# Order of transfers and decoding steps before the first attention slot, and a finished row of w3 @ w_out in three slots instead of two

## The chip, the cores and the metric

The kernel runs on one core of a Trainium2 chip. The metric is the device time of one execution in microseconds (us). The core has a matrix engine (TensorE, PE in the profile, with its weight loads as PEld), a vector engine (VectorE, DVE), a scalar engine (ScalarE, ACT), a general engine (GpSimd, POOL) and a queue engine (SyncE, SP) that here issues all transfers. Each engine runs its own instructions strictly in order and waits for the others by semaphores. Matrix products are accumulated in PSUM banks; everything else lies in SBUF.

## The reference

Three stages follow each other: clustered attention over 2 x 8 heads of 768 x 64, a product MLP, and a second MLP with softplus.

```python
mask = q_assign[:, :, :, None] == k_assign[:, :, None, :]   # nearest of 16 centroids, by head
scores = np.where(mask, scale * np.matmul(q, k.transpose(0, 1, 3, 2)), -1000000000.0)
attn = np.exp(scores - np.max(scores, axis=-1, keepdims=True))
attn = attn / (np.sum(attn, axis=-1, keepdims=True) + 1e-09)
x = np.matmul(attn, v)               # (1536, 512) after the heads are put side by side
h = (x @ w1) * (x @ w2) @ w3         # w1, w2: 512 x 1024; w3: 1024 x 1024
y = h @ w_out                        # w_out: 1024 x 512
g = softplus(y @ w_in)               # w_in: 512 x 2048
out = g @ w_o2                       # 2048 x 512
```

The MLP weights come as float64. The kernel reads them as pairs of 32-bit words and builds float32 from them.

## The kernel before

**Attention in slots.** Heads are taken in eight pairs. The loop `for s in range(NSLOT + ML + AL)` has 106 slots, six for each of the 16 heads and ten more for the lag. Slot s computes the scores of 128 queries against all keys on PE (`mx_pe`, line 592), takes their extremum on DVE (`mx_red`, line 601), and, nine slots behind, computes the scores transposed (`st_pe`, line 622), their exponential on ACT (`st_exp`, line 629) and, one slot further behind, the product with v (`av_pe`, line 637). The score buffers `mbank` and `sbank` are single: `mx_pe` of a slot waits for the reduction of the slot before, `st_pe` for the exponential of the slot before.

**Preparation of the next pair.** The tables `PE` and `EV` lay the work for pair pi over the slots of the pairs before it, by slot minus 12 pi. This text calls s modulo 12 the position. Position 0 loads q and k (`load_qk`); 4 to 7 square and sum them on POOL and DVE; 8 to 11 turn q and k on PE and copy them on ACT into the tiles H and L (`t1_pe`, `t1_ev`, lines 299 and 310), half j = 0 in 8 and 9, half j = 1 in 10 and 11. Position 9 also has `norm_root` (lines 274 and 275) on ACT. Positions 1 to 5 of the next twelve compare with the centroids, and 7 ends with `back_pe` and `back_ev` (tile sg). The copies from H, L and sg into the operands of the score products are transfers on SP: `t_dma(pi, j)` has seven, `m_dma(pi, j)` two. They stand at position 4 (`t_dma` for j = 0) and 8 (`m_dma` 0, `t_dma` 1, `m_dma` 1: eleven transfers in a row). H and L have one buffer for each j, so `t1_ev` of a pair for j = 1, at position 10, waits until `t_dma` for j = 1 of the pair before has been read out.

**The product w3 @ w_out.** Beside the attention the kernel computes w3 @ w_out once, in 24 jobs n (`wseq`): four halves-of-w_out rows ("o"), eight w3 rows ("3"), and the same again for the second half g = 1. Job n begins at step k = 3n, and one step runs in each slot. The table `WT` says which letter runs at which step after 3n: A, b, c, d decode a weight (A on ACT, b, c, d on DVE; d also issues the next load, since three raw buffers are there); s splits w_out on ACT and POOL; T turns w3 on PE (line 488); h and l split it on ACT and DVE; m is the accumulation on PE (`w3_acc`, line 507, 12 products); p adds the first half's row on DVE for g = 1 (`w3_add`, line 515); q copies the leading part on ACT (`w3_out`, tiles w3oh and w3p); e takes the remainder on DVE and gives the PSUM bank back (`w3_end`). Within a slot the letters h, l, p, q, e come after `mx_red` and before `st_exp`; A, b, c, d, s after `st_exp`; T and m at the end of the slot. The bank for T, m and the turns of the preparation is one of three (`rbank`), taken first in, first out.

**Before the first slot.** A hand-written list prepares pair 0 and loads weights; then eight rounds `r` from -20 to -13 prepare pair 1, with one decoding step each (`w_next`), and further steps follow until `wk[0]` is 14. So slot 0 starts at step 14 and slot s runs step s + 14. When `wk[0]` reaches `NWSTEP` = 82 (slot 67) the first three weights of the first MLP are loaded (`feed.load(3)`, 1.5 MB, tile w12r); they are decoded later by `feed.take`.

Of the kernel before, what the change touches and what calls it, by code (L numbers as in the profile page):

```python
# [22 lines left out]
def f32(ap):  # L23
    return ap.bitcast(F32)
# [3 lines left out]
def fused_kernel(ctx: ExitStack, tc, q, k, v, centroids, w1, w2, w3, wo, w_in, w_o2, out):  # L28
# [11 lines left out]
    QC = S // P  # L40
# [33 lines left out]
    def load_w(pl, src, cols, name):  # L74

        wide = src.dtype != F32
        t = pl.tile([P, 1024], I32, tag="raw", name=name)
        if not wide:
            t = t.bitcast(F32)[:, :512]
        tv = t if cols is None else t.rearrange("p (c f) -> p c f", c=cols)  # L80
        dma_in(tv, src.bitcast(I32) if wide else src)
        return t
# [103 lines left out]
    def load_qk(pi):  # L186
        if pi >= NPAIR:
            return
        b, h0 = divmod(2 * pi, H)
        r = ap1.tile([P, 2, QC, 2, D], F32, tag="rawqk", name=f"rawqk{pi}")  # L190
        for ni, src in enumerate((q, k)):
            for j in range(2):
                dma_in(r[:, j, :, ni, :], src[b, h0 + j].rearrange("(p c) d -> p c d", p=P))
        QK[pi] = r

    def centroid_load():
        PR["cw"] = ap1.tile([P, D], F32, name="cw")
        dma_in(PR["cw"], centroids.rearrange("h c d -> (h c) d"))

    def centroid_prep():  # L200
        cw = PR["cw"]
        sq = ap1.tile([P, D], F32, name="csq")
        s = ap1.tile([P, 8], F32, name="cs")
        nc.scalar.activation(sq, cw, AF.Square, accum_out=s[:, 0:1])
        nc.gpsimd.tensor_tensor(
            out=s[:, 1:2], in0=s[:, 0:1], in1=half_c, op=ALU.pow
        )

        nc.vector.tensor_scalar_max(s[:, 2:3], s[:, 1:2], 1e-30)
        nc.vector.reciprocal(s[:, 3:4], s[:, 2:3])  # L210
        nc.vector.scalar_tensor_tensor(
            out=s[:, 4:5], in0=s[:, 3:4], scalar=s[:, 0:1], in1=s[:, 2:3],
            op0=ALU.mult, op1=ALU.add,
        )
        nc.vector.tensor_scalar(
            out=s[:, 5:6], in0=s[:, 4:5], scalar1=0.5, scalar2=1e-6,
            op0=ALU.mult, op1=ALU.add,
        )
        nc.vector.reciprocal(s[:, 6:7], s[:, 5:6])
        cn = PR["cn"] = ap1.tile([P, 2, D], F32, name="cn")  # L220
        for i in range(2):
            nc.vector.tensor_scalar(
                out=cn[:, i, :], in0=cw, scalar1=s[:, 6:7], scalar2=None, op0=ALU.mult
            )
# [22 lines left out]
    def norm_sq(pi, j):  # L247
        sq = ring.tile([P, QC, 2, D], F32, tag="w3k", name=f"sq{pi}_{j}")
        if pi >= 2:
            nc.gpsimd.tensor_tensor(out=sq, in0=QK[pi][:, j], in1=QK[pi][:, j], op=ALU.mult)  # L250
        else:
            nc.scalar.activation(sq, QK[pi][:, j], AF.Square)
        PR["sq", j] = sq
# [63 lines left out]
    def t_dma(pi, j):  # L317

        hd = 2 * pi + j
        a, l = f32(PR["H", j]), f32(PR["L", j])
        qt = QT[hd] = apT.tile([P, 2, S], F32R, tag="q", name=f"q{hd}")
        kt = KT[hd] = apT.tile([P, 2, S], F32R, tag="k", name=f"k{hd}")
        nc.gpsimd.memset(f32(kt[96:97, 1, :]), 1.0)
        dma = nc.sync.dma_start
        dma(f32(qt[:D]), a[:D].unsqueeze(1).to_broadcast([D, 2, S]))
        dma(f32(kt[:D, 0, :]), a[D:])
        dma(f32(kt[:D, 1, :]), l[D:])
        for n in range(2):  # L330
            dma(f32(qt[D : D + 32, n, :]), l[32 * n : 32 * n + 32])
            dma(f32(kt[D : D + 32, n, :]), a[D + 32 * n : D + 32 * n + 32])
# [78 lines left out]
    def m_dma(pi, j):  # L411
        for ni, d in enumerate((QT, KT)):
            o = 64 * ni + 32 * j
            nc.sync.dma_start(f32(d[2 * pi + j][96:, 0, :]), f32(PR["sg"][o : o + 32, :]))
# [9 lines left out]
    NW = len(wseq)  # L424
    wnext = [0]

    def w_load():
        n = wnext[0]
        if n < NW:
            k, i, g = wseq[n]  # L430
            if k == "o":
                r = g * NK + i
                src = wo[r * P : (r + 1) * P, :]
            else:
                src = w3[i * P : (i + 1) * P, g * 512 : (g + 1) * 512]
            W3["r", n] = load_w(raws, src, None, f"w3r{n}")
            wnext[0] += 1
# [90 lines left out]
    def w3_end(n):  # L528
# [7 lines left out]

    WT = {
        "o": {0: "Ab", 1: "c", 2: "d", 5: "s"},
        "3": {0: "Ab", 1: "c", 2: "d", 3: "T", 4: "hl", 7: "m", 8: "pq", 9: "e"},
    }  # L540
    WF = {
        "A": w_scale, "b": lambda n: w_bits(n, 0), "c": lambda n: w_bits(n, 1),
# [4 lines left out]
    def w_step(k, kinds):  # L547
        for n in range(max(0, k // 3 - 3), min(NW, k // 3 + 1)):
            for x in WT[wseq[n][0]].get(k - 3 * n, ""):
                if x in kinds:  # L550
                    WF[x](n)
# [3 lines left out]
    def load_v(pi):  # L555

        if pi < NPAIR:
            b, h0 = divmod(2 * pi, H)
            for j in range(2):
                t = xp.tile([P, QC, 2 * D], F32, tag="x", name=f"v{pi}_{j}")  # L560
                nc.gpsimd.memset(t[:, :, D * (1 - j) : D * (2 - j)], 1.0)
                dma_in(
                    t[:, :, D * j : D * j + D], v[b, h0 + j].rearrange("(p c) d -> p c d", p=P)
                )
                V[2 * pi + j] = t
# [16 lines left out]
    NH = B * H  # L582
    NSLOT = NH * QC
    ML = 9
    AL = 1
# [90 lines left out]
    def x_norm(u):  # L676
        g, hf = divmod(u, 2)
        b, h = divmod(g, H)
        if b not in XT:
            XT[b] = xp_.tile([P, CC, S], F32, tag="x1", name="xT1")  # L680
        rs = slice(D * (h % 2), D * (h % 2) + D)
        cs = slice(hf * HALF, (hf + 1) * HALF)
        nc.gpsimd.tensor_tensor(  # L683
            out=XT[b][rs, h // 2, cs],
            in0=TT.pop(u)[rs], in1=R[g // 2][rs, cs], op=ALU.mult,
        )
# [137 lines left out]


    WALL = "AbcdsThlmpqe"
    W0 = 14
    wk = [0]

    def w_next(kinds=WALL):  # L830
        w_step(wk[0], kinds)
        wk[0] += 1

    with tc.manual_schedule():
        centroid_load()
        load_qk(0)
        for _ in range(3):
            w_load()
        load_v(0)
        centroid_prep()  # L840
        t1_pe(0, 0)
        t1_pe(0, 1)
        t1_ev(0, 0)
        norm_sq(0, 0)
        t1_ev(0, 1)
        centroid_turn()
        t1_pe(0, 2)
        t1_pe(0, 3)
        t1_ev(0, 2)
        norm_sq(0, 1)  # L850
        t1_ev(0, 3)
        t_dma(0, 0)
        t_dma(0, 1)
        load_qk(1)
        load_v(1)
        norm_sum(0, 0)
        sims_pe(0, 0)
        sims_ev(0, 0)
        norm_sum(0, 1)
        norm_root(0)  # L860
        sims_pe(0, 1)
        sims_ev(0, 1)
        w_next()
        norm_rec(0, 0)
        norm_rec(0, 1)
        simsT_pe(0)
        w_next()
        norm_rec(0, 2)
        w_next()
        assign(0, 0)  # L870
        assign(0, 1)
        w_next()
        back_pe(0)
        back_ev(0)
        m_dma(0, 0)
        m_dma(0, 1)
        for r in range(-20, -2 * QC):
            steps(PE, r + 2 * QC)
            steps(EV, r + 2 * QC)
            if wk[0] < W0:  # L880
                w_next()
        while wk[0] < W0:
            w_next()
        for s in range(NSLOT + ML + AL):
            j = s - ML
            a = j - AL
            if s < NSLOT:
                mx_pe(s)
                mx_red(s)
            if s and s % QC == 0 and s <= NSLOT:  # L890
                m_row(s // QC - 1)
            w_step(wk[0], "hlpqe")
            if a > 0 and a % 3 == 0:
                av_ev(a // 3 - 1)
            steps(PE, s)
            steps(EV, s)
            if 0 <= j < NSLOT:
                st_pe(j)
                st_exp(j)
            w_step(wk[0], "Abcds")  # L900
            if 0 <= a:
                av_pe(a)
            w_step(wk[0], "Tm")
            wk[0] += 1

            for g in range(NH):
                r = s - (ML + AL + QC * g + QC - 1)
                if r in (2, 4, 6):
                    r_ev(g, r // 2 - 1)
                if r == 8:  # L910
                    x_norm(2 * g)
                    x_norm(2 * g + 1)
            if wk[0] == NWSTEP:
                feed.load(3)
                assert s < ML + AL + QC * NH // 2 + QC + 6
            if s == NSLOT + 1:
                feed.take(2)
                taken += 2
# [179 lines left out]
```

## Time and profile before

| | us |
|---|---|
| median of 3 runs | 882.47 (881.14 to 884.43) |
| profiled execution | 882.9 |
| its span | 881.1 |
| PE busy | 813.7 (92%) |
| DVE busy | 498.7 (57%) |
| ACT busy | 413.2 (47%) |
| POOL busy | 242.8 (28%) |
| first reduction of slot 0 begins | 42.70 |
| last reduction of slot 95 begins | 367.3 |

The busy share of PE says little by itself, since a product on half the clock is busy twice as long. The page's line PEclk gives the granted clock in tenths of full speed in 40 slices of 22 us; its two levels are 1.2 and 2.4 GHz (0.50 and 1.00). Views used below: the waits (who waited for whom), the timeline (instructions in order of time with the idle time before them and what ended it), the windows (busy time and granted clock of a stretch), and the chain (the work that ended last, followed back).

### The profile page before, as it was taken

What the parts mean: (1) busy time and instruction counts of PE and PEld (TensorE: products, weight loads), DVE (VectorE), ACT (ScalarE), POOL (GpSimd) and SP (SyncE); (2) the same over time, 40 slices, a digit from 0 to 9 for tenths busy, and PEclk for the clock granted to TensorE, in tenths of its full rate; (3) what the DMA queues carried; (4) which work ended last, traced back from release to release, by engine and by line L of the source; (5) the groups of instructions that cost most, each with busy time, mean ns of one, the idle gap of its engine ahead of it and who ended that gap; (6) DMA issues with size and microseconds to landing.
All of it is one profiled execution on the core that took longest, in us unless ns stands there. A gap on an engine that the chain in (4) does not pass through costs nothing.

```text
span 881.1 us, 11317 instructions
## 1 busy us (share of the span) xinstructions
PE 813.7 (92%) x4033; PEld 704.9 (80%) x4033; DVE 498.7 (57%) x903; ACT 413.2 (47%) x763; POOL 242.8 (28%) x249
## 2 busy tenths in 40 slices
PE   4289999899999699989999999999979999999998
PEld 3167777677777577759999999998878999899886
DVE  6585657585755455439642324775996445445442
ACT  3325454444444444455542423665556545545543
POOL 2431215241414111145410011342443222222221
PEclk9579999899999899999999999999999999999999
DMA  9774455654535634036410111450200000000001
GB/s 225 171 191 133 116 145 140 159 147 105 126 82 114 156 82 109 11 101 202 155 48 10 41 48 48 147 189 1 96 24 1 37 1 1 37 1 0 36 1 37
DMA packets 77832, 76.47 MB, mean 87 GB/s; under 512 B 46416, under 2 KB 62928, under 8 KB 77776
## 3 DMA queue, kind: packets, MB, share of 16 engines
q1 hardware_dynamic: 77776, 75.75, 31.8%
q8 instruction: 32, 0.52, 0.2%
q14 instruction: 24, 0.20, 0.1%
HBM read 50.41 MB, written 3.24 MB: 61 GB/s over the span
## 4 chain that ended last, share of the span: by engine, by line
PE 72%; DVE 11%; DMA 6%; issue 4%; ACT 3%; SPq 2%; POOL 2%; DVEq 0%; ACTq 0%; POOLq 0%
PE avb L637 11%; PE sb L622 6%; PE mb L1027 6%; PE sb L784 6%; PE rb L784 6%; PE sb L983 6%; PE rb L983 6%; PE rb L507 4%; PE mb L592 3%; PE mb L806 3%; PE rb L1027 3%; PE avb L1027 3%; DMA q<-H 2%; PE rb L806 2%; PE avb L806 2%
## 5 line engine op out<-in xcount | busy, mean ns | idle before, releaser
L601 DVE TENSOR_REDUCE mn<-mb 128x1 f32<-128x768 f32 x96 | 91.6, 954 | 110.4 <-PE mb L592 110.0
L637 PE MATMUL avb<-E,v 128*128 128x384 f32 x384 | 144.7, 500 | 0.0
L66 POOL TENSOR_TENSOR ln<-ln,u 128x384 f32<-128x384 f32 x64 | 67.1, 1050 | 179.3 <-DVE ln L1007 173.8
L622 PE MATMUL sb<-q,k 128*128 128x384 f32 (+1 forms) x384 | 92.0, 362 | 19.2 <-ACT E L629 19.2
L629 ACT ACTIVATE E<-sb 128x768 f32<-128x768 f32 x96 | 77.6, 808 | 50.0 <-PE sb L622 49.0
L637 PEld LDWEIGHTS avb<-E,v 128*128 128x128 f32 x384 | 73.1, 195 | 28.1 <-issue 2.4
L622 PEld LDWEIGHTS sb<-q,k 128*128 128x128 f32 (+1 forms) x384 | 67.5, 195 | 26.6 <-ACT E L629 23.7
L592 PE MATMUL mb<-k,q 128*128 128x384 f32 x192 | 70.4, 449 | 12.2 <-DVE mn L601 11.4
L983 PE MATMUL sb<-ys,wh_i 128*128 128x384 f32 x256 | 72.5, 344 | 7.5 <-ACT t L994 6.9
L983 PE MATMUL rb<-ys,wh_i 128*128 128x384 f32 x256 | 70.6, 337 | 0.0
L784 PE MATMUL sb<-xs,wh 128*128 128x384 f32 x256 | 68.6, 339 | 1.7 <-DVE ab L793 1.7
L784 PE MATMUL rb<-xs,wh 128*128 128x384 f32 x256 | 68.0, 336 | 0.0
L996 DVE TENSOR_SCALAR u<-t 128x384 f32<-128x384 f32 x64 | 24.3, 379 | 73.1 <-ACT t L995 72.7
L592 PEld LDWEIGHTS mb<-k,q 128*128 128x128 f32 x192 | 36.0, 200 | 33.1 <-DVE mn L601 15.8
L983 PEld LDWEIGHTS sb<-ys,wh_i 128*128 128x128 f32 x256 | 47.7, 191 | 11.6 <-ACT t L994 8.9
L66 POOL TENSOR_TENSOR wl_o<-d_o,wh_o 128x512 fp32r<-128x512 f32 x16 | 20.8, 1301 | 127.8 <-ACT wh_o L61 124.2
L1004 DVE SCALAR_TENSOR_TENSOR u<-u,t 128x384 f32<-128x384 f32 x64 | 37.6, 588 | 23.7 <-ACT ln L1002 23.5
L784 PEld LDWEIGHTS sb<-xs,wh 128*128 128x128 f32 x256 | 46.3, 188 | 3.5 <-DVE ab L793 2.3
L683 POOL TENSOR_TENSOR xT<-t,R 64x384 f32<-64x384 f32 x32 | 34.3, 1090 | 49.9 <-DMA R<-rd 43.7
L983 PEld LDWEIGHTS rb<-ys,wh_i 128*128 128x128 f32 x256 | 46.9, 188 | 1.3
L784 PEld LDWEIGHTS rb<-xs,wh 128*128 128x128 f32 x256 | 46.5, 188 | 0.1
L1002 ACT ACTIVATE ln<-u 128x384 f32<-128x384 f32 x64 | 33.3, 520 | 24.7 <-DVE u L996 24.4
(178 smaller groups left out, 1884.4 us busy)
## 6 DMA issues: line engine op xcount, KB each, us to landing
w3r<-in_moe_w_dram SPq DMA_DIRECT2D x16, 512.0 KB
w12r<-in_moe_w_dram SPq DMA_DIRECT2D x16, 512.0 KB
wir<-in_moe_w_in_dram SPq DMA_DIRECT2D x16, 512.0 KB
wor<-in_moe_w_out_dram SPq DMA_DIRECT2D x16, 512.0 KB
q<-H SPq DMA_DIRECT2D x16, 384.0 KB
w3r<-in_moe_w_out_dram SPq DMA_DIRECT2D x8, 512.0 KB
rawqk<-in_q_dram SPq DMA_DIRECT2D x16, 192.0 KB
rawqk<-in_k_dram SPq DMA_DIRECT2D x16, 192.0 KB
```

Source lines behind the costliest of these rows:

```text
L66: nc.gpsimd.tensor_tensor(out=o, in0=i, in1=hi, op=ALU.subtract)
L507: nc.tensor.matmul(m, a[:, ks], bb, start=(mc == 0 and x == 0), stop=(mc == NK - 1 and x == 2))
L592: nc.tensor.matmul(mbank[:, hf, :HALF], QT[g][:, 0, c * P : (c + 1) * P], KT[g][:, 0, hf * HALF : (hf + 1) * HALF], start=True, stop=True,)
L601: nc.vector.tensor_reduce(out=MN[g][:, c : c + 1], in_=mbank[:, :, :HALF], op=ALU.min, axis=AX.XY)
L622: nc.tensor.matmul(sbank[:, i, :HALF], KT[g][: P - 31 * n, n, ks], QT[g][: P - 31 * n, n, qs], start=(n == 0), stop=(n == 1),)
L629: nc.scalar.activation(E[j], sbank[:, :, :HALF], AF.Exp, scale=-1.0)
L637: nc.tensor.matmul(avbank[:, :HALF], V[g][:, 2 * kp + i, :], e[:, i, :], start=(kp == 0 and i == 0), stop=(kp == 2 and i == 1),)
L784: nc.tensor.matmul(bk[:, :BLK], a[:, sl], bb, start=(n == 0), stop=(n == 3 * CC - 1))
L806: nc.tensor.matmul(ybank[e][:, :BLK], a[:, es], bb, start=(fc == 0 and n == 0), stop=(fc == NFC - 1 and n == 2),)
L983: nc.tensor.matmul(hbank[(bl * NF2 + fc) % 4][:, :BLK], a[:, sl], bb, start=(n == 0), stop=(n == 3 * CC - 1))
L1004: nc.vector.scalar_tensor_tensor(out=u, in0=u, scalar=-1.0, in1=t, op0=ALU.add, op1=ALU.subtract)
L1027: nc.tensor.matmul(ob, a[:, sl], bb, start=(fc == 0 and n == 0), stop=(fc == NF2 - 1 and n == 2),)
```

## The change

- Before the first slot: two weights are loaded at first instead of three, and v of pair 0 not there. `load_qk(1)` moves ahead of `t_dma(0, 1)`, which itself moves behind `m_dma(0, 0)`. The third weight and `load_v(0)` come after `m_dma(0, 1)`, and `load_v(1)` after the rounds.
- Only A and b of job 0 stay ahead of the rounds. `W0` becomes 9: slot s runs step s + 9, five steps less than before, and every letter of the stream moves by five slots.
- The letters p, q and e of a finished row stand at steps 8, 9 and 10 instead of 8, 8 and 9.
- One assertion goes and one is added; they issue nothing.

```diff
-        "3": {0: "Ab", 1: "c", 2: "d", 3: "T", 4: "hl", 7: "m", 8: "pq", 9: "e"},
+        "3": {0: "Ab", 1: "c", 2: "d", 3: "T", 4: "hl", 7: "m", 8: "p", 9: "q", 10: "e"},
...
-    W0 = 14
+    W0 = 9
...
         centroid_load()
         load_qk(0)
-        for _ in range(3):
-            w_load()
-        load_v(0)
+        w_load()
+        w_load()
         centroid_prep()
...
         t_dma(0, 0)
-        t_dma(0, 1)
         load_qk(1)
-        load_v(1)
...
         sims_ev(0, 1)
-        w_next()
         norm_rec(0, 0)
         norm_rec(0, 1)
         simsT_pe(0)
-        w_next()
         norm_rec(0, 2)
-        w_next()
+        w_step(0, "A")
+        w_step(0, "b")
         assign(0, 0)
         assign(0, 1)
-        w_next()
         back_pe(0)
         back_ev(0)
         m_dma(0, 0)
+        t_dma(0, 1)
         m_dma(0, 1)
+        w_load()
+        load_v(0)
+        wk[0] = 1
         for r in range(-20, -2 * QC):
             steps(PE, r + 2 * QC)
             steps(EV, r + 2 * QC)
             if wk[0] < W0:
                 w_next()
-        while wk[0] < W0:
-            w_next()
+        load_v(1)
```

## Rows read from the trace of the kernel before

**Rows 1.** The page, granted clock in 40 slices of the span.

```profile
PEclk9579999899999899999999999999999999999999
```

**Rows 2.** Waits of PE from 64 to 400: us in total, times, longest us.

```profile
PE sb L622 <- ACT E L629: 19.2, 12, 6.7
PE mb L592 <- DVE mn L601: 0.8, 2, 0.5
```

**Rows 3.** Timeline of PE, three stretches: start us, us, what, in brackets idle before.

```profile
163.09 1.65 PE L622 MATMUL sb<-q,k 128*128 128x384 f32 x4 [2.73 <-ACT E L629]
...
205.82 0.97 PE L622 MATMUL sb<-q,k 128*128 128x384 f32 x4 [2.07 <-ACT E L629]
...
305.28 1.65 PE L622 MATMUL sb<-q,k 128*128 128x384 f32 x4 [6.73 <-ACT E L629]
```

**Rows 4.** Windows: stretch and length in us, busy by engine, PEclk, DMA share, GB/s.

```profile
19.20:49.90 30.70, 10.86 (x40) 8.57 (x40) 19.34 (x32) 11.37 (x21) 11.86 (x13) 0.50 0.83 187
...
162.50:169.40 6.90, 6.32 (x16) 4.91 (x17) 4.39 (x8) 2.65 (x5) 2.47 (x4) 0.51 0.26 90
206.90:210.40 3.50, 3.50 (x11) 2.33 (x10) 0.86 (x3) 1.72 (x3) 1.11 (x3) 0.51 0.40 151
302.50:309.40 6.90, 4.12 (x9) 2.91 (x10) 2.16 (x4) 2.56 (x4) 3.11 (x6) 0.51 0.21 45
```

**Rows 5.** Timeline of ACT in the same stretches.

```profile
161.75 0.58 ACT L310 ACTIVATE H<-rb,qkcol 128x384 fp32r<-128x384 f32 x1 [3.69 <-DMA k<-H]
...
202.36 0.60 ACT L61 ACTIVATE w3oh<-rb 128x512 fp32r<-128x512 f32 x1 [5.15 <-DVE rb L515]
...
297.65 0.70 ACT L63 ACTIVATE w12r<-w12r 128x512 f32<-128x512 f32 x1 [1.72 <-DMA w12r<-in_moe_w_dram]
303.95 0.58 ACT L310 ACTIVATE H<-rb,qkcol 128x384 fp32r<-128x384 f32 x1 [5.59 <-DMA k<-sg]
```

**Rows 6.** Timeline of SP in the first and the last of these stretches.

```profile
152.58 0.56 SPq L414 DMA_DIRECT2D q<-sg  x1
...
158.92 0.59 SPq L332 DMA_DIRECT2D k<-H  x1
...
288.72 1.74 SPq L81 DMA_DIRECT2D w12r<-in_moe_w_dram  x3
```

**Rows 7.** Chain of work in order of time, from 64 on: start us, us, what.

```profile
72.10 0.44 PE rb L488 x4
...
73.22 0.72 PE sb L622 x4
73.93 1.29 PE avb L637 x4
75.23 2.78 PE rb L507 x12
...
158.92 2.72 DMA k<-H
...
392.38 4.63 DMA w12r<-in_moe_w_dram
```

**Rows 8.** Timeline of all engines from 14 to 67, the start.

```profile
14.28 0.60 SPq L332 DMA_DIRECT2D k<-H  x1
...
22.02 0.90 ACT L408 ACTIVATE sg<-rb,bigcol 128x768 fp32r<-128x768 bf16 x1 [5.59 <-PE rb L402]
...
27.76 0.57 SPq L414 DMA_DIRECT2D q<-sg  x1
27.83 0.84 ACT L252 ACTIVATE sq<-rawqk 128x768 f32<-128x768 f32 x1 [4.91 <-DMA rawqk<-in_k_dram]
...
36.47 0.42 DVE L457 TENSOR_SCALAR w3r<-w3r 128x512 int32<-128x512 int32 x1
...
42.70 0.95 DVE L601 TENSOR_REDUCE mn<-mb 128x1 f32<-128x768 f32 x1
...
66.58 0.94 PE L622 MATMUL sb<-q,k 128*128 128x384 f32 x4
```

More of the change, by code (lines that the diff above doesn't have):

```diff
@@ L679, in x_norm @@
         if b not in XT:
+            assert wk[0] > 3 * NW + 4
             XT[b] = xp_.tile([P, CC, S], F32, tag="x1", name="xT1")
@@ L914, in fused_kernel @@
                 feed.load(3)
-                assert s < ML + AL + QC * NH // 2 + QC + 6
             if s == NSLOT + 1:
```

## The prediction

> **What bounds the kernel now.** I read the page first. PE is busy 92% of the span (the table above), and in most of the 40 slices its clock is at or near full [rows 1]; from the first slots on the kernel is bound by PE, and a gain can come only from PE's idle time, from its time at half clock, or from what lies ahead of the stretch that PE fills. So the next view is PE's waits from 64 us on: 19.2 us in 12 waits of the transposed scores for the exponential before, 0.8 us for the reduction, and nothing else [rows 2]. The timeline shows that four of the 12 hold most of it: 2.73, 2.07 and 6.73 us [rows 3], and at 255.94 one that repeats the second to the digit; counted along the 96 reductions of line 601 these are slots 35, 46, 58 and 71. Three of the four are followed by a stretch at 0.51 of the clock, in which PE was busy 6.32, 3.50 and 4.12 us [rows 4]; at full clock the same work takes half, so they cost 3.16, 1.75 and 2.06 us more. The four, with their clock, are the prize: A = 2.73 + 3.16 = 5.9, B = 2.07 + 1.75 = 3.8, B' = 2.07, C = 6.73 + 2.06 = 8.8, in all 20.6 us.
>
> Then ACT in these stretches, because each wait is for an exponential. ACT runs in order, so what it waited for just before is the cause. In A it waited 3.69 us to write H, for `t_dma` to have read the old one; in C 5.59 us for the same kind of thing; in B it waited 5.15 us for the sum p of line 515 before the copy q, and the exponential stood behind q [rows 5]; B' has the same row 50 us later. SP shows why the transfers were late: in A the eleven transfers of position 8 start at 152.58, and the last of `t_dma` is issued at 158.92 [rows 6] and lands 2.72 us later [rows 7]. In C the three weights of `feed.load(3)`, 1.5 MB, are issued at 288.72, right ahead of the eleven [rows 6].
>
> **The change part by part.**
>
> *p, q, e in three slots (B, B').* Before, the accumulation m ends a slot; in the next, p waits for DVE's reduction, which waits for PE's scores behind m; q waits for p on ACT; the exponential waits behind q. That is the 5.15 us. With q one slot later its operand is long there, and p comes behind a reduction that waits for the same PE work, so DVE waits no longer than it did. Cost of the move: none of instructions; e gives the bank back one slot later, which is weighed below. B and B' go: -5.9 us. Next late there is the exponential's own scores, which PE itself sets.
>
> *Five steps later (C).* `feed.load(3)` moves from slot 67 to 72, position 0, behind `m_row`'s transfer of that slot. Until position 4 of the next pair only small transfers and v follow on SP, so the eleven of slot 68 have a free queue. C goes: -8.8. What is left there: ACT still meets one early decode of w12r, for which it waited 1.72 us [rows 5]. It should move along with the load and wait again, now with nothing else late: +1.7 (from 0 to the 5.6 of the row below it).
>
> *Five steps later (A).* The accumulations, 2.78 us each [rows 7], stood in slots 2 modulo 3, thus at positions 2, 5, 8, 11; now in 1 modulo 3, at 1, 4, 7, 10. One at 7 lets SP begin the eleven while PE is still in 7; one at the end of 10 fills PE while the exponential is late. Jobs 12 to 15 have none, so slots without accumulation were 27 to 40 and will be 32 to 45. Slot 34 (now with one in 31) and slot 46 (now with one of its own) each get 2.78 us of cover against a wait of 2.73. I take A as gone, -5.9, and leave 1.6 us for remnants in slots 34, 46 and 70 (none, to the whole 5.9 if the lag moves with the slots).
>
> *The start.* Before, pair 1's q and k are there at 27.83 and the copies of sg are issued at 27.76, though sg is ready at 22.92 [rows 8]: both stand in SP behind `t_dma(0, 1)`, weights and v. Now load_qk(1) follows `t_dma(0, 0)`, issued by 14.88 [rows 8], and needs about 5 us (4.63 for the slowest of the nearest kind [rows 7]): some 7 us earlier. On the other side `t_dma(0, 1)` waits in SP behind sg, and the third weight behind it. sg, with about 0.5 us of decoding less ahead of it, at 22.4; then eleven issues (nine took 6.9 from 152.58 to 159.51 [rows 6], so 8.5), load issued at 30.9, landed 2.7 to 4.6 later (the two transfers of [rows 7]): 33.6 to 35.5. ACT and DVE need it for job 2 and stand in line behind it with the last two turns. From the like point, 36.47, to slot 0 at 42.70 [rows 8] DVE needed 6.2 us, of which two steps (1.1) now come later: slot 0 at 38.7 to 40.6, say 39.2, 3.5 us earlier. (Not earlier at all if the squares of pair 1 have to wait for the buffer of sg, which SP now empties last: 42.7.) Slots 0 to 8 took 23.9 us, 42.70 to 66.58 [rows 8], with two accumulations among them, of which the later stood on the path: 23.9 - 2.8 = 21.1. PE's full stretch then begins at 60.3, 6.3 earlier. But two accumulations and two turns (0.44 each [rows 7]) that lay in the thin start now lie in the full stretch: 2 x (2.78 + 0.44) = 6.4. Net 0, from -4 to +5.
>
> Its clock is part of that span: between 19.2 and 49.9 it stood at 0.50, with PE busy 10.86 of 30.70 us [rows 4], and rose only after some dense us in slots 1 to 3. With two accumulations less the slots up to 8 are thinner. The Trainium skill ("TensorE: Matmul & The Clock Gate", "What's actually happening") says the gate follows how busy PE has lately been, and only knows half and full. The trace agrees in these stretches. By that rule the full stretch could begin at half clock, which this change makes likelier; a stretch like the one in A would then cost 3.2 us, an estimate from that row.
>
> *Rest.* The bank: in the second half the accumulation of job n takes the bank that e of job n-1 gives back early in the same slot. PE has 0.72 + 1.29 us [rows 7] of other products between the scores and it, DVE a reduction of 0.95 [rows 8] and e (0.6, as q [rows 5]), so e is done in time unless DVE is late; remnants +0.5. Each of the moved decoding letters keeps its neighbours; nothing is added. The MLP stages keep their order: 0, within 2 us either way.
>
> **Sum.** -20.6 + 1.7 + 1.6 + 0.5 + 0 = -16.8. The profiled span of 881.1 becomes 864.3; the execution took 882.9, 1.8 more, so 866.1; the median was 0.4 below that execution: 865.7. I say 865.5.
>
> **The rivals.**
>
> 1. *SP's lag moves with the slots.* The transfers at position 8 are still eleven, and ACT still waits for them at 10. If the cover by accumulations does not reach, A stays (5.9) and the decode of w12r costs up to 5.6 instead of 1.7: 865.5 + 5.9 - 1.6 + 3.9 = 874. For it: eleven issues of 0.6 to 0.7 us each are longer than two slots. Against: of the slots at position 10 with an accumulation beside the eleven, none is among the four waits except through q. Chance 0.13.
>
> 2. *The start gives nothing and costs.* Slot 0 not earlier (buffer of sg), and the full stretch begins at half clock: 865.5 + 3.5 + 3.2, about 872. Chance 0.10.
>
> 3. *Slower: e becomes the wait.* With one slot more, the bank is free only after DVE's reduction and e in the slot of the next accumulation. By the terms above PE reaches that accumulation 2.0 us after the scores and DVE ends e 1.6 us after them; it decides once DVE starts a slot more than 0.4 us late. If DVE were 2 us late in the seven slots of jobs 17 to 23, PE would stand 7 x 2 us, each followed by 1.75 of clock as in B: +26, thus 892. Against: PE waited for the reduction only twice, 0.8 us in all [rows 2]. Chance 0.05.
>
> 4. *It does not do what it says:* the waits only change place, each as large as before, with 6.4 us of PE work moved against an earlier start of the same size. 880 to 884. Chance 0.06.
>
> **How the numbers follow.** My forecast, 857 to 872, has 0.66. The 8 in 10: from 856 (remnants zero, start -4, and some of the small waits gone too) to 879, which takes in rivals 1 and 2. Faster by over 0.5% (about what a measurement of this kernel tells from no change) means below 878.1: forecast, rivals 1 and 2, less a little for costs that add up, 0.86. Within: 0.08. Slower, above 886.9: 0.06.
>
> **What would show it.** Right: in PE's waits from 64 to 400 the 19.2 us fall to about 5; ACT has no copy w3oh waiting 5 us for line 515; no stretch of half clock inside the attention slots after the start; `feed.load(3)` in slot 72 with PE going on; the first reduction near 39 and the first transposed scores near 60. Wrong in A: H waits over 3 us at slot 46 or 34 with PE idle behind it. Wrong in the start: first reduction at 42 or later. Wrong in the bank: line 507 waits for DVE. What I least trust is the landing of the third weight and where the early decode of w12r stands.

## The result and the profile after

The changed kernel takes 867.38 us in the median (867.09 to 868.11, 4 runs) against 883.3 (881.14 to 884.43, 4 runs) for the kernel before, measured beside it; the ratio is 0.9824, interval 0.9802 to 0.9846. The prediction was 865.5, with 856 to 879 as its range.

The waits of PE from 64 to 400 (us in total, times, longest), which answer to [rows 2]:

```profile
PE sb L622 <- ACT E L629: 8.7, 8, 2.3
PE avb L637 <- issue: 1.0, 2, 0.5
PE avb L637 <- ACT t L61: 0.4, 1, 0.4
```

The 19.2 us for the exponential are 8.7, and half of these lie behind the last slot. Two lines are new: the product with v of line 637 waits, which it did not before.

The timeline of PE at slots 35, 46, 71 and behind the last slot (start, us, what, idle before):

```profile
160.99 0.97 PE L622 MATMUL sb<-q,k 128*128 128x384 f32 x4 [1.10 <-ACT E L629]
...
194.12 1.53 PE L637 MATMUL avb<-E,v 128*128 128x384 f32 x4 [0.48 <-issue]
...
291.22 0.98 PE L622 MATMUL sb<-q,k 128*128 128x384 f32 x4 [1.28 <-ACT E L629]
...
361.63 0.97 PE L622 MATMUL sb<-q,k 128*128 128x384 f32 x4 [1.97 <-ACT E L629]
...
370.36 0.98 PE L622 MATMUL sb<-q,k 128*128 128x384 f32 x4 [2.28 <-ACT E L629]
```

Of [rows 3], the 2.73 of slot 35 is 1.10 and the 6.73 of slot 71 is 1.28; of the two waits of 2.07 at slots 46 and 58 nothing is left at the exponential. At slot 46, and likewise at 58, the product with v waits 0.48 instead.

The windows (busy time by engine, then the granted clock, DMA share, GB/s), which answer to [rows 4]:

```profile
50.70:60.90 10.20, 6.96 (x26) 5.04 (x27) 9.48 (x17) 2.91 (x5) 7.22 (x7) 0.50 0.80 181
60.90:371.50 310.60, 300.24 (x1407) 230.90 (x1407) 189.05 (x317) 150.92 (x255) 86.41 (x100) 1.00 0.49 123
371.50:375.00 3.50, 3.50 (x9) 2.58 (x8) 2.16 (x4) 1.29 (x3) 0.74 (x1) 0.51 0.00 0
```

From 60.9 to 371.5 the clock never falls. The three stretches of half clock inside the slots are gone; one ends the thin start, one lies behind the last slot. The kernel before had such stretches there too: 60.2 to 63.6, and 377.6 to 381.0, both at 0.50.

Where the time went, stretch by stretch: the beginnings of the scores of line 592, counted slot by slot in the two traces, and of the last product with v.

| from, to | before, us | after, us | difference | prediction |
|---|---|---|---|---|
| start to slot 32 | 150.50 | 150.19 | -0.3 | 0 |
| slot 32 to 38 (A) | 23.74 | 18.32 | -5.4 | -5.4 |
| slot 38 to 68 (B, B') | 114.53 | 111.94 | -2.6 | -4.9 |
| slot 68 to 72 (C) | 19.95 | 12.57 | -7.4 | -8.3 |
| slot 72 to 95 | 57.76 | 57.43 | -0.3 | +1.7 |
| slot 95 to the last product with v | 26.43 | 27.80 | +1.4 | 0 |
| rest | 488.20 | 487.43 | -0.8 | 0 |
| span | 881.1 | 865.7 | -15.4 | -16.8 |

(The 1.6 of remnants is shared here among slots 34, 46 and 70, and the 0.5 for the bank stands with B, B'.) The sum was missed by 1.4 us, but the terms less evenly: two were too good by 2.3 and 0.9, one cost did not come (1.7), and the stretch behind slot 95 is 1.4 longer. That the total came so close is in part luck, since these errors have both signs.

Each figure of the table is from one execution, and the runs below have further profiles of the same stretches. Slots 32 to 38 took 22.4 in three runs that keep the accumulations where they were (e1, e2, e3): half clock lasted 3.4 us there instead of 6.8. So A is worth 4.0 to 5.4. Slots 38 to 68 took 113.2 and 112.9 in two runs with the old letters at the old place (e2, e3), with both waits of 2.07 and no half clock behind them. So B and B' are worth 0.9 to 2.6. C is firm: it took 20.4 in e1 and e3, which leave the loads in slot 67, so the gain is 7.4 to 7.9. The 1.4 behind slot 95 is not the change's: a second profile of the changed kernel (e11) has 26.45 there, before 26.43.

### The profile page after: what moved, and what is told of

It is laid out like the page before. It is cut to its first block, busy times and chain, and to the rows that moved or that the text cites. A ratio compares the mean times of both kernels' runs of the same rounds, so it can differ in the third digit from the quotient of the medians.

```text
span 865.7 us, 11313 instructions
## 1 busy us (share of the span) xinstructions
PE 809.1 (93%) x4033; PEld 701.2 (81%) x4033; DVE 499.8 (58%) x903; ACT 411.4 (48%) x763; POOL 244.7 (28%) x249
## 4 chain that ended last, share of the span: by engine, by line
PE 78%; DVE 9%; issue 5%; ACT 3%; SPq 2%; DMA 1%; POOL 1%; ACTq 0%; DVEq 0%; POOLq 0%
PE avb L637 12%; PE sb L981 7%; PE mb L1025 7%; PE sb L622 7%; PE rb L981 6%; PE sb L785 6%; PE rb L785 6%; PE rb L507 5%; PE mb L592 4%; PE mb L807 3%; PE avb L1025 3%; PE rb L1025 3%; PE rb L807 2%; PE avb L807 2%; PE rb L345 1%
## 5 line engine op out<-in xcount | busy, mean ns | idle before, releaser
L637 PE MATMUL avb<-E,v 128*128 128x384 f32 x384 | 141.6, 490 | 1.6 <-issue 1.0
L637 PEld LDWEIGHTS avb<-E,v 128*128 128x128 f32 x384 | 71.0, 190 | 30.6 <-ACT t L61 2.3
L592 PE MATMUL mb<-k,q 128*128 128x384 f32 x192 | 69.4, 444 | 15.4 <-DVE mn L601 15.4
```

Source lines behind the costliest of these rows:

```text
L592: nc.tensor.matmul(mbank[:, hf, :HALF], QT[g][:, 0, c * P : (c + 1) * P], KT[g][:, 0, hf * HALF : (hf + 1) * HALF], start=True, stop=True,)
L637: nc.tensor.matmul(avbank[:, :HALF], V[g][:, 2 * kp + i, :], e[:, i, :], start=(kp == 0 and i == 0), stop=(kp == 2 and i == 1),)
```

## The experiments

My theory was the sum's own: four waits with their clock, each gone for its own reason, and a start that balances. The rivals were that one common cause (five slots later) does it all, or that the new order of transfers at the start does. Times are medians, and ratios are to the kernel before, measured beside each group. The runs are numbered e1 to e11.

**The parts of the change alone (the kernel before: 881.66).**

The letters only (e1):

```diff
-... 8: "pq", 9: "e"},
+... 8: "p", 9: "q", 10: "e"},
```

> The kernel before with p, q, e at steps 8, 9, 10 and nothing else. My theory (the copy q waited for the sum p on ACT, and two exponentials stood behind it): the two PE waits at slots 46 and 58 go, 2 x 2.07, and the 1.75 of half clock behind the first, 5.9 in all, less about 1 for what stands next: 877 to 879 against 883. Rival (the split does nothing alone, the waits went because the letters moved to other slots): 882 to 884.

Measured: 878.76, ratio 0.9962 (0.9935 to 0.9988). The timeline of PE at slots 46, 53 and 58:

```profile
203.44 0.80 PE L622 MATMUL sb<-q,k 128*128 128x384 f32 x3 [0.86 <-ACT E L629]
...
233.32 0.50 PE L507 MATMUL rb<-woh,w3th 128*128 128x512 f32 x1 [0.96 <-DVE w3ol L69]
...
251.70 0.62 PE L622 MATMUL sb<-q,k 128*128 128x384 f32 x2 [0.86 <-ACT E L629]
```

The theory had the right kind and the wrong size. Each 2.07 falls to 0.86, no stretch of half clock follows, and slots 38 to 68 are 3.3 us shorter (111.24 against 114.53); against e2 and e3, which have the two waits without half clock, 1.6 to 2.0. The median moved by 2.9 instead of 4 to 6. The row between shows rival 3 of the prediction in small: one accumulation waits 0.96 us for e. It stays at one.

The three loads only, in slot 72 (e2):

```diff
-            if wk[0] == NWSTEP:
+            if s == 72:
                 feed.load(3)
```

> The kernel before with the three loads of the first MLP's weights in slot 72 instead of 67, nothing else. Theory (the loads stood ahead of the eleven transfers of position 8): the wait of 6.73 at slot 71 falls to what is left in the kernel after there (1.3) up to a wait as in slot 35 (2.7), with less or no half clock: 5 to 7.5 faster, 876 to 878. Rival (the eleven transfers themselves are the wait, as in slot 35): 4.5 to 6 remain of 8.8, so 879 to 881.

Measured: 875.25, ratio 0.9916 (0.9888 to 0.9943), thus 6.4 faster. PE's wait at slot 71:

```profile
299.24 0.97 PE L622 MATMUL sb<-q,k 128*128 128x384 f32 x4 [1.32 <-ACT E L629]
```

The 1.5 MB ahead of the eleven transfers were the cause of C, and the rival falls: without them 1.32 us is left, not a wait as in slot 35.

The order of transfers only (e3: the new list before the rounds, but fourteen steps before slot 0 and the old letters; the edit is shown against the changed kernel):

```diff
-... 8: "p", 9: "q", 10: "e"},
+... 8: "pq", 9: "e"},
...
-    W0 = 9
+    W0 = 14
...
+        while wk[0] < W0:
+            w_next()
         load_v(1)
```

> The new order of transfers before the first slot, with fourteen steps before slot 0 and the letters as before. Theory: slot 0 as late as before, near 43, because five more decoding steps stand on DVE behind the third weight; the four waits stay in slots 35, 46, 58, 71: 881 to 885. Rival (the order itself brings a gain at the start of 3 us or more): first reduction at 40 or earlier, 879 or less.

Measured: 882.87, ratio 1.0012 (0.9987 to 1.0037): no difference. DVE's timeline at the first reduction:

```profile
42.61 0.52 DVE L457 TENSOR_SCALAR w3r<-w3r 128x512 int32<-128x512 int32 x1
43.23 0.69 DVE L461 SCALAR_TENSOR_TENSOR w3r<-w3r 128x512 int32<-128x512 int32 x1
43.84 0.95 DVE L601 TENSOR_REDUCE mn<-mb 128x1 f32<-128x768 f32 x1
```

Slot 0 begins at 43.84, 1.1 later than before [rows 8], with decoding right up to it. It is no later than in e2 (43.77), whose start is that of the kernel before: two profiles of one start differ by as much. So the new order brings slot 0 no nearer by itself.

The steps and letters only, in the old order of transfers (e4):

```diff
-... 8: "pq", 9: "e"},
+... 8: "p", 9: "q", 10: "e"},
...
-    W0 = 14
+    W0 = 9
```

> The old order of transfers, with nine steps before slot 0 and the new letters. Theory: the five steps fewer bring the earlier start and move the accumulations and the loads, so this has nearly all of the gain: first reduction near 39, waits at 35, 46, 58, 71 gone, 866 to 869. Rival (the new order of transfers is needed for the gain at the start): first reduction at 42 or later and 870 or more.

Measured: 869.0, ratio 0.9851 (0.9807 to 0.9894), which overlaps the interval of the whole change. Its first reduction stands earlier than in the changed kernel (38.01 against 39.76), and slot 35 looks the same:

```profile
38.01 0.94 DVE L601 TENSOR_REDUCE mn<-mb 128x1 f32<-128x768 f32 x1
...
159.95 0.80 PE L622 MATMUL sb<-q,k 128*128 128x384 f32 x3 [1.13 <-ACT E L629]
```

So the five steps and the letters carry the change, and no gain of the new order can be seen: e3 and e4 say so from both sides.

**Parts put back or moved, on the changed kernel (867.38; 866.71 when it was run again beside the last two).** The kernel before, beside e5 to e8: 882.81.

Twelve steps instead of nine (e5: the same positions, other slots; the three loads fall into slot 69, right behind the eleven transfers):

```diff
-    W0 = 9
+    W0 = 12
...
+        while wk[0] < W0:
+            w_next()
         load_v(1)
```

> The changed kernel with twelve steps before slot 0 instead of nine: the letters stand at the same positions as in the changed kernel, but the last accumulation of the first half falls into slot 28 instead of 31, the last of all into 64 instead of 67. Theory (an accumulation at position 7 or 10 covers the eleven transfers): slots 34 and 70 lose their cover, PE waits about 2.7 us at slot 35 and again at 71, some of it followed by half clock; covered still at 46 and 58: 3 to 9 slower than the changed kernel, 870 to 876. Rival (the positions alone do it): no wait over 1.3 at slots 35 and 71, 866 to 869.

Measured: 876.1, ratio 0.9924 (0.9902 to 0.9947). PE's waits at slots 35 and 71:

```profile
167.30 0.98 PE L622 MATMUL sb<-q,k 128*128 128x384 f32 x4 [2.93 <-ACT E L629]
...
297.94 0.98 PE L622 MATMUL sb<-q,k 128*128 128x384 f32 x4 [1.35 <-ACT E L629]
```

Slot 35: the theory. With the last accumulation of the first half in slot 28, the wait is back at its old length, at the same positions; half clock does not follow it. Slot 71: the rival. There the cover is gone too, and the wait is 1.35 without it and 1.28 with it (1.32 in the kernel with the loads in slot 72). So the accumulation is worth 1.8 us at slot 35 and nothing at 71.

What it does at slot 35 can be read from DVE and SP, first in the changed kernel (slot 32 begins at 150.19), then here (at 154.37):

```profile
147.35 0.19 DVE L665 RECIPROCAL r<-r 128x6 f32<-128x6 f32 x1
147.56 0.35 SPq L667 DMA_DIRECT2D rd<-r  x1
148.01 0.55 SPq L414 DMA_DIRECT2D q<-sg  x1
...
156.82 0.59 SPq L332 DMA_DIRECT2D k<-H  x1
```

```profile
153.77 1.08 DVE L461 SCALAR_TENSOR_TENSOR w3r<-w3r 128x512 int32<-128x512 int32 x1
...
155.79 0.19 DVE L665 RECIPROCAL r<-r 128x6 f32<-128x6 f32 x1
156.01 0.35 SPq L667 DMA_DIRECT2D rd<-r  x1
156.45 0.55 SPq L414 DMA_DIRECT2D q<-sg  x1
...
162.81 0.59 SPq L332 DMA_DIRECT2D k<-H  x1
```

SP has a small transfer of the inverted row sums (`rd`, line 667) right ahead of the eleven, and issues it as soon as DVE has done line 665. With an accumulation at the end of slot 31, DVE gets there 2.7 us before slot 32 begins; without it 1.6 us after, straight behind decoding letters. The last of `t_dma` is issued 6.6 us after the beginning of slot 32 in the one and 8.4 in the other (8.4 in before, too), and these 1.8 us are as much as the difference of the two waits. At slot 68 no weight is decoded any more: in e5 DVE ends line 665 at 286.76, just before the slot begins at 286.81, without any cover. That the letters make up the difference between the two places is likely, but no run takes them out.

The other part of the loss is the start. Slot 0 begins at 42.80, as in the kernel before (42.70), but one accumulation less lies in the thin stretch, and slot 32 comes 4.2 us later than in the profile after, and 1.8 to 3.9 later than in three profiles of the old start (150.50 to 152.53). That fits the moved PE work, 2.78 + 0.44, without the earlier start that pays for it.

The copy t ahead of the letters (e6):

```diff
-            w_step(wk[0], "hlpqe")
             if a > 0 and a % 3 == 0:
                 av_ev(a // 3 - 1)
+            w_step(wk[0], "hlpqe")
```

> The changed kernel with the copy t of the product with v ahead of the letters h, l, p, q, e in each slot. Theory (in the changed kernel h stands on ACT ahead of t in the same slots, and the next product with v waits for t, since its bank is single): the waits of line 637 at slots 22, 46 and 58 (0.43 to 0.48 in the profile, 0.7 counted from the transposed scores) go, about 2 us faster: 864 to 866. Rival (what is missing of the second and third wait is DVE's work in these slots): 867 to 868, waits of the same length under another name.

Measured: 865.54, ratio 0.9816 (0.9775 to 0.9858). ACT's timeline at slot 46, first in the changed kernel, then in this one:

```profile
192.51 0.66 ACT L63 ACTIVATE w3r<-w3r 128x512 f32<-128x512 f32 x1
193.06 0.58 ACT L61 ACTIVATE w3th<-rb 128x512 fp32r<-128x512 f32 x1
193.54 0.49 ACT L61 ACTIVATE t<-avb 128x384 f32<-128x384 f32 x1
```

```profile
191.12 0.66 ACT L63 ACTIVATE w3r<-w3r 128x512 f32<-128x512 f32 x1
191.68 0.48 ACT L61 ACTIVATE t<-avb 128x384 f32<-128x384 f32 x1
192.05 0.59 ACT L61 ACTIVATE w3th<-rb 128x512 fp32r<-128x512 f32 x1
```

With t first, PE's waits from 64 to 400 no longer name line 637:

```profile
PE sb L622 <- ACT E L629: 8.5, 8, 2.0
PE mb L592 <- DVE mn L601: 0.3, 1, 0.3
PE sb L785 <- DVE ab L794: 0.3, 1, 0.3
```

Slots 38 to 68 take 110.48 instead of 111.94 (and 110.33 instead of 112.23 in e10 against e9, below, the same edit once more), so at least 1.5 us of the missing gain is this: the move by five slots put h into the slots of t, and the product with v, whose bank is single, waits for t. The time moves the same way, by 1.8, but its interval overlaps that of the changed kernel.

The three loads back in slot 67 (e7):

```diff
-            if wk[0] == NWSTEP:
+            if s == 67:
                 feed.load(3)
```

> The changed kernel with the three loads of the first MLP's weights in slot 67, as before, instead of 72. Theory: they stand again ahead of the eleven transfers; PE waits 4 to 6.7 us at slot 71 (one accumulation, 2.78, now lies in slot 67 and covers part), with half clock behind it: 4 to 7.5 slower, 871 to 875. Rival (the wait went through the cover by the accumulation alone): 867 to 869.

Measured: 873.33, ratio 0.9912 (0.9879 to 0.9946). PE at slots 70 and 71:

```profile
290.65 0.97 PE L622 MATMUL sb<-q,k 128*128 128x384 f32 x4 [1.69 <-ACT E L629]
...
296.82 1.01 PE L622 MATMUL sb<-q,k 128*128 128x384 f32 x2 [3.22 <-ACT E L629]
```

As the theory has it, 1.69 + 3.22 of wait, and half clock from 295.7 to 302.5: slots 68 to 72 take 17.5 instead of 12.6.

The old letters (e8):

```diff
-... 8: "p", 9: "q", 10: "e"},
+... 8: "pq", 9: "e"},
```

> The changed kernel with p, q, e at steps 8, 8, 9 as before. My prediction as it stands (the split takes the two waits of 2.07 away): they come back with the clock, 2 to 6 slower, 869 to 873. Rival (the five slots alone do it: the slots in which q waits are now 2 modulo 3, so they no longer fall on position 9, where norm_root stands in front of the exponential too): no wait over 0.9 at any exponential of the second half, 866 to 869.

Measured: 873.89, ratio 0.9907 (0.9876 to 0.9938). The size is a little above that of the prediction, the shape that of neither side. PE's waits for the exponential from 64 to 400:

```profile
PE sb L622 <- ACT E L629: 11.7, 13, 2.6
```

No wait of 2.07 returns; the largest inside the slots is 1.25. But slots 38 to 68 take 116.8 instead of 111.9, with waits of 0.4 to 1.3 at six slots (48, 54, 57, 58, 60, 66); all but 58 come right behind a slot with p and q, where ACT's copy q again waits for line 515, 5.0 to 5.5 us in seven of its eight rows. So the split is needed at the new place too, and is worth more there (6.5 against 2.9). And the rival of one common cause falls: the five slots without the split give some 9 us of the 15 to 16.

**Two edits on top (the kernel before: 881.44).** `t_dma(0, 1)` right behind `load_qk(1)` (e9):

```diff
         load_qk(1)
+        t_dma(0, 1)
         norm_sum(0, 0)
...
         m_dma(0, 0)
-        t_dma(0, 1)
         m_dma(0, 1)
```

> The changed kernel with t_dma(0, 1) right behind load_qk(1), ahead of m_dma(0, 0). In the changed kernel SP stands idle there from about 18 to 23 us, waiting for sg. Theory (slot 0 is set by the landing of the third weight, for which ACT and DVE waited 2.87 and 3.39 us, and which the seven transfers hold up): the weight lands near 30, slot 0 begins near 36.4 instead of 39.8, the full stretch of PE 3.4 earlier; 863 to 866 against 867.4. Rival (the start is set by something else, the clock or the pace of slots 0 to 8): first reduction earlier, but the transposed scores of slot 9 still at 60 and the time at 867.

Measured: 865.94, ratio 0.9825 (0.9795 to 0.9855). The reason for the edit is in the timelines of SP, ACT and DVE of the changed kernel at the start, which answer to [rows 8]: SP is idle from 17.76 to 23.17, and the third weight, issued at 31.32, is waited for.

```profile
16.42 1.34 SPq L193 DMA_DIRECT2D rawqk<-in_k_dram  x2
23.17 0.58 SPq L414 DMA_DIRECT2D q<-sg  x1
...
31.32 0.59 SPq L81 DMA_DIRECT2D w3r<-in_moe_w_out_dram  x1
...
35.11 0.69 ACT L63 ACTIVATE w3r<-w3r 128x512 f32<-128x512 f32 x1 [2.87 <-DMA w3r<-in_moe_w_out_dram]
...
39.76 0.94 DVE L601 TENSOR_REDUCE mn<-mb 128x1 f32<-128x768 f32 x1
...
60.64 1.09 PE L622 MATMUL sb<-q,k 128*128 128x384 f32 x4
```

With the edit the first reduction and the first transposed scores stand at:

```profile
36.65 0.94 DVE L601 TENSOR_REDUCE mn<-mb 128x1 f32<-128x768 f32 x1
...
57.24 0.93 PE L622 MATMUL sb<-q,k 128*128 128x384 f32 x3
```

ACT and DVE no longer wait for the third weight. Both rows are some 3 us earlier, and so is slot 32: 146.79 against 150.19, and 148.80 to 152.31 in five profiles of the changed start (after, e6, e7, e8, e11). What holds up the third weight holds up the whole start. The median moved by 0.8 to 1.4 only, with runs from 864.16 to 868.97; the gain in time is less sure than that in the trace.

Both edits (e10), and the changed kernel once more beside them (e11):

> The changed kernel with both edits: t_dma(0, 1) right behind load_qk(1), and the copy t ahead of the letters. If the two are apart from each other, as the theory has it, their gains add: 2 for t and up to 3.4 for the start, 861 to 865. Rival (a common limit): no better than the better of the two.

> The changed kernel as it is, on the same chip as the two others, so that they can be compared directly: 866 to 869.

Measured: 863.24, ratio 0.9789 (0.9763 to 0.9815), against 866.71, ratio 0.9825 (0.9802 to 0.9848). The intervals just overlap; by the medians both edits give 3.5 of the 5.4 hoped for. It is the fastest version here. Its waits of PE from 64 to 400 are one line:

```profile
PE sb L622 <- ACT E L629: 6.9, 7, 2.0
```

## Why the prediction was right, point by point

**What bounds the kernel.** Right. The gain was in PE's waits for the exponential and the clock behind them, and the sum of four waits gave the size; how the terms share it is told below.

**p, q, e (B, B').** Right in kind, the term mis-sized: 5.9 forecast, less 1.0 of costs; 2.6 measured, and 0.9 to 1.3 against e2 and e3. Of the 5.9, 1.75 was the half clock behind slot 46, which only the trace of before has. The step that failed is "next late there is the exponential's own scores". Next late was, first, `norm_root` in ACT's queue. It stands right ahead of the exponential at position 9 and waits for the norms from DVE (line 273). Its row in before, and in e1:

```profile
204.59 0.22 ACT L274 ACTIVATE nrm<-nrm 128x24 f32<-128x24 f32 x1 [1.16 <-DVE nrm L273]
...
202.21 0.22 ACT L274 ACTIVATE nrm<-nrm 128x24 f32<-128x24 f32 x1 [1.68 <-DVE nrm L273]
```

With the letters alone 0.86 us of PE's wait is left at each of the two slots. It also tells why PE waited at two places only: in before q waits 5.15 us for p four times (202.36, 229.40, 252.49, 277.42), but only the first and the third fall on position 9. So q alone was not the cause of the 2.07, as the prediction had it. Second, t behind h, 1.5 us, which I had not seen though I listed that the letters move to 1 modulo 3, where `av_ev` stands too; "each of the moved decoding letters keeps its neighbours" was wrong. Third, one turn of 0.44 more lies in this stretch after than before (that of job 16), which the table then gives back in the stretch ahead. Of the 3.3 between 5.9 and 2.6 that leaves 1.4; 0.3 is the wait at slot 47 shown below, and about 1 I can't place.

**The loads (C).** Right: 7.4 measured in the slots of C, 6.4 in the median of the loads alone, and put back they cost what was said. The decode of w12r moved along as forecast, and ACT did wait for it again:

```profile
295.11 1.52 SPq L81 DMA_DIRECT2D w12r<-in_moe_w_dram  x3
...
303.10 0.70 ACT L63 ACTIVATE w12r<-w12r 128x512 f32<-128x512 f32 x1 [1.47 <-DMA w12r<-in_moe_w_dram]
```

The price of 1.7 was wrong: PE's slots there kept their length, since the wait of 1.47 lay beside a long slot of PE (position 3 has the turns of the comparison).

**A.** Right in kind, and the reason holds for slot 35: an accumulation at position 7 lets SP begin the eleven before slot 32 (e5). The size, 5.4 as forecast, is right for this pair of traces; 3.16 of it was forecast for the clock, and against the three profiles with a shorter half clock A is 4.0. In either, 0.44 is the turn named above. At slot 46 ACT's copy into H waits 4.08 us (the profile names nothing that it waited for), longer than the 3.69 of before at slot 34, and PE went on, as the prediction put it: it runs the accumulation meanwhile, and the transposed scores of slot 47 wait 0.32.

```profile
198.10 0.58 ACT L310 ACTIVATE H<-rb,qkcol 128x384 fp32r<-128x384 f32 x1 [4.08 <-issue]
...
199.44 0.80 PE L622 MATMUL sb<-q,k 128*128 128x384 f32 x3 [0.32 <-ACT E L629]
```

No run takes the cover away at slot 46 alone. At slot 71 it was not needed.

**The start.** Slot 0 at 39.76 (39.2 forecast, 38.7 to 40.6), the first transposed scores at 60.64 (60.3), balance -0.3 (0). Slot 0 is firm: 39.58 to 39.94 in five profiles, 42.70 to 43.77 in three of the old start. The balance is not: slot 32 begins at 148.80 to 152.31 in the five and at 150.50 to 152.53 in the three. The fear for the clock came true: in all five profiles half clock lasted past the first transposed scores, by 0.3 us in the profile after and up to 5 (e7: scores at 62.04, half clock to 67.0), while in the three of the old start it ended 2 us or more ahead of them. The credit was misplaced in part. I gave room to q and k of pair 1 being there 7 us earlier. e4 reaches slot 0 at 38.01 without it: what the new order gains there, it loses at the third weight (e9 takes that loss away, 36.65). The five steps alone bring the earlier start.

**The rest.** Rival 3 shows once, with 0.96, in e1, and not after. Behind the last slot, "0, within 2 us" was 1.4 in this pair of profiles: the second wait there is 2.28 instead of 0.90, with the half clock behind it. In the trace of before this wait was:

```profile
386.49 0.97 PE L622 MATMUL sb<-q,k 128*128 128x384 f32 x4 [0.90 <-ACT E L629]
```

Before, the half clock came one wait earlier and its loss lay beside ACT's wait for w12r (1.40 at 385.06); after, it came behind that wait (2.79 at 368.94), and nothing covers it. Which of the two it is changes from one execution to the next: in e11, the same kernel, the half clock came behind the first wait (364.2 to 367.6), the second is 0.99, and the stretch takes 26.45. It takes 27.5 to 28.1 in the five profiles that have half clock behind the second wait, and 25.7 to 27.0 in the eight others.

## What to carry to other kernels

When a stream of side work is moved by some slots against a periodic main loop, list for every slot class what now stands in one engine's queue with it, and not only which long pieces move: the long pieces gave the gain, a copy of 0.58 us in front of another took 1.5 us back. Look too at what stands directly ahead of the piece that waits: the same wait of 5.15 us for p cost PE 2.07 in two slots and nothing in two others. A bulk load belongs where nothing latency-bound follows it in the same queue for as long as it takes to land; that one line was worth 6.4 us alone. And work moved out of a thin start into the full stretch costs about its whole length (3.2 us by the sum, 1.8 to 3.9 in e5), so an earlier start has to pay for it first. A difference between two profiles is checked against a third: the terms here that rest on the clock moved by 1.3 to 1.7 us between profiles of the same stretch.

## What the runs showed of the hardware

Whether half clock follows a wait is not settled by the wait's length here: 2.07 us was followed by 0.51 at 205.82 and by full clock at 255.94 in the same execution, and by full clock at both places in e2 and e3; after, 1.97 at 361.63 by full clock and 2.28 at 370.36 by 0.51. Nor is its duration: behind the wait of 2.7 at slot 35 it was 6.8 us in before and 3.4 in e1, e2 and e3, and behind the wait of 2.93 in e5 there was none. And at the start two profiles of the changed kernel had half clock from 50.7 to 60.9 and from 50.2 to 63.9, with slot 32 at 150.19 and 151.67. So a term of 1.5 to 3 us that comes from the clock is uncertain by its whole size, and the medians of the kernel before, 881.44 to 883.3 in four groups of runs, differ by as much as the smaller of these.
